# Linear attention with an MLP on one core: the feature map as min(exp, max(x + 1, 1)) and a new order of work in batches 0, 2 and 3

## The chip, the cores and the metric

The kernel runs on one core of one Trainium2 chip. The metric is the device time of one execution in microseconds (us); where several executions are given, the median counts. One further execution was taken by the hardware profiler, and all lines of profile below come from it. The engines are named as in the profile: PE is the matrix engine (PEld its weight loads), DVE the vector engine, ACT the scalar engine, POOL is GpSimd, and SP the queue that issues most of the transfers (DMA).

## The reference

```python
def phi(x):
    return np.where(x > 0, x, np.exp(x) - 1.0) + 1.0
q_p, k_p = (phi(q), phi(k))                    # q, k, v: 8 batches, 8 heads, 576 x 64
kv = np.einsum('bhsd,bhse->bhde', k_p, v)
z = np.sum(k_p, axis=2)
num = np.einsum('bhsd,bhde->bhse', q_p, kv)
den = np.einsum('bhsd,bhd->bhs', q_p, z)[..., None] + 1e-06
x = num / den                                  # then 4608 tokens x 512
h = x @ w_in                                   # 512 x 2048
g = 0.5 * h * (1.0 + np.tanh(c * (h + 0.044715 * h * h * h)))
out = g @ w_out                                # 2048 x 512
```

The feature map phi(x) is x + 1 for positive x and exp(x) otherwise. Two ways to write it matter here: max(x, 0) + min(exp(x), 1), and min(exp(x), max(x + 1, 1)). For positive x, exp(x) is above x + 1; for others, exp(x) is at most 1.

## The kernel before

**Tiles.** The 576 tokens of a batch are split into a main part of 512 tokens, held as 128 partitions with C = 4 chunks each, and a rest of 64. The rests of two batches share a tile of 128 partitions (k_r, v_r, q_r). The main tile of q, k or v is `[128, 8 heads, 4 x 64]` in fp32: within a head, the four chunks lie side by side. The feature maps k_p and q_p are `[128, 4, 8, 64]` in bf16: a chunk with all its heads is contiguous, because matmuls and transposes take pairs of heads (128 columns) of one chunk. All tiles loaded from memory, batches and weights alike, rotate through six buffers (`pld`, tag "ld"). A new load waits until the tile six loads back is read for the last time.

**Attention of a batch.** `exp_main` (L164) or a piece like L341 stores exp(x) in bf16 on ACT, in the layout of the input. `phi_into` (L169) does the rest on the DVE: one minimum with 1 over exp (L171), then for each chunk one operation with two tensor inputs, max(x, 0) + e (L175). `cast_v` (L202) puts v in bf16 beside a column of ones, `cast_vr` (L208) the rest of v. `kv_mm` (L213) multiplies k_p by v for each of four pairs of heads, five matmuls a pair. The ones' column gives z. `kv_evac` (L234) copies the result from PSUM into block-diagonal matrices (kvbd). q_p is transposed, on PE (L247, L336) or by a DMA transpose (`qtr`), and `nab_mm` (L251) forms numerator and denominator in one. `nab_evac` (L260) takes the reciprocal and multiplies (x, bf16). x is transposed once more into xt, the input of the first layer: by PE and a copy (`pe_tx`, L374 to L383) in batches 0 to 2, by a DMA transpose (`tx`, L487) in later ones.

**The two layers.** For each main part j of 512 tokens, and a ninth part made of all rests, `first_half(j)` (L657) runs m = 0 to 15: four matmuls of 128x512 for 128 hidden units (`first_mm`, L301) and a gelu on ACT (L675). Then `second_half(j)` (L703) runs 16 slots of four matmuls (L718) and copies outputs out. `first_mm_early` (L310) does the first 256 tokens of one m ahead of its time, at the end of the stage before, into a PSUM buffer; `first_half` then does the other 256.

**The order of work.** It is written out by hand. Each engine runs its instructions in the order of the program. `at(phase, j, slot, fn)` appends a function to a list that is run after slot `slot` of first_half(j) (phase 1) or second_half(j) (phase 2); functions of one slot run in the order in which they were appended. `plan_second`, `plan_third` (L586) and `plan_prepare` with `plan_attention` place the attention of batches 1, 2 and 3 to 7 so: batch 2 is prepared within second_half(1), batch 3 from second_half(1) to first_half(2). exp and gelu use different tables of ACT, so a stretch of exps has a table load at both ends.

**The head.** Batch 0 has no layer work to lie beside. PE is fed with filler matmuls there (`keep_warm(n)`, L325: 2n matmuls of 252 columns on zeros). The code from L339 to L407 gives the order: four exps for halves of the heads of k and q, `phi_into` for the same halves, `transpose_q` 0 and 1, fillers, the rest of k (`phi_rest_half`), casts of v, `transpose_q` 2 and 3, fillers, then twice `kv_mm` for two pairs and `kv_evac`. Between the two rounds stand two casts of v (L358, L359). `kv_evac` copies one half on the DVE, the other on ACT, one after the other.

**PSUM.** Two pools: `ps_ho` with four buffers of a bank (h_ps, o_ps, fillers, some transposes) and `ps_a` with two buffers of two banks (kv_ps, n_ps, and in j < 2 the first-layer results of m = 12 to 15, two to a buffer, L665 to L668). Both rotate in order of allocation. A matmul into a buffer waits for the reader of what was in it.

Of the kernel before, what the change touches and what calls it, by code (L numbers as in the profile page):

```python
# [15 lines left out]
def kernel(  # L16
# [17 lines left out]
    C = 4  # L34
# [128 lines left out]

    def exp_main(name, b):  # L164
        e = pe.tile([P, H, C * D], BF16, name=name + "_e")
        nc.scalar.activation(e, ld[name, b], AF.Exp)  # L166
        return e

    def phi_into(xp, x, e, hs):  # L169

        nc.vector.tensor_scalar(e[:, hs], e[:, hs], 1.0, None, op0=ALU.min)  # L171
        xv = x.rearrange("p h (c d) -> p c h d", d=D)
        ev = e.rearrange("p h (c d) -> p c h d", d=D)
        for c in range(xp.shape[1]):
            nc.vector.scalar_tensor_tensor(  # L175
                xp[:, c, hs, :], xv[:, c, hs, :], 0.0, ev[:, c, hs, :],
                op0=ALU.max, op1=ALU.add,
            )

    def phi_of(x, e, name):  # L180
        xp = pphi.tile([P, x.shape[2] // D, H, D], BF16, name=name)
        phi_into(xp, x, e, slice(0, H))
        return xp

    def phi_rest(name, m):
        x = ld[name, m]
        e = pe.tile([P, H, D], BF16, name=f"{name}_e{m % 2 if name == 'qr' else ''}")
        nc.scalar.activation(e, x, AF.Exp)
        return lambda: phi.__setitem__((name, m), phi_of(x, e, name + "_p"))

    def exp_rest_half(name, e, s):
        r = slice(REST * s, REST * (s + 1))
        nc.scalar.activation(e[r], ld[name, 0][r], AF.Exp)

    def phi_rest_half(name, e, s):
        r = slice(REST * s, REST * (s + 1))
        nc.vector.tensor_scalar(e[r], e[r], 1.0, None, op0=ALU.min)
        nc.vector.scalar_tensor_tensor(
            phi[name, 0][r, 0], ld[name, 0][r], 0.0, e[r], op0=ALU.max, op1=ALU.add
        )  # L200
# [114 lines left out]
    ke = pe.tile([P, H, C * D], BF16, name="k_e")  # L315
    qe = pe.tile([P, H, C * D], BF16, name="q_e")
    kre = pe.tile([P, H, D], BF16, name="kr_e")
# [21 lines left out]
    for n, e in (("k", ke), ("q", qe)):  # L339
        for s in halves:  # L340
            nc.scalar.activation(e[:, s], ld[n, 0][:, s], AF.Exp)  # L341
    exp_rest_half("kr", kre, 0)
    keep_warm(36)
    for n, xp, e in (("k", kp, ke), ("q", qp, qe)):
        for s in halves:
            phi_into(xp, ld[n, 0], e, s)
# [4 lines left out]
    cast_v(0, nc.scalar.copy, halves[0])  # L351
    cast_vr(0, (0,))
    for i in range(2, NP):
        transpose_q(i, nc.scalar.copy)
    keep_warm(2)
    for h in range(2):
        if h == 1:
            cast_v(0, nc.vector.tensor_copy, slice(4, 6))  # L358
            cast_v(0, nc.scalar.copy, slice(6, 8))  # L359
# [36 lines left out]
    kre1 = pe.tile([P, H, D], BF16, name="kr_e")  # L396
# [125 lines left out]
    def plan_second():  # L522
# [4 lines left out]
        def exps():  # L527
            box["q"] = pe.tile([P, H, C * D], BF16, name="q_e")
            for s in halves:
                nc.scalar.activation(box["q"][:, s], ld["q", b][:, s], AF.Exp)  # L530
            gelu_table()

        def phis():
            phi["q", b] = pphi.tile([P, C, H, D], BF16, name="q_p")
            for s in halves:
                phi_into(phi["q", b], ld["q", b], box["q"], s)
# [49 lines left out]
    def plan_third():  # L586
# [4 lines left out]
        def exps():  # L591
            box["k"] = exp_main("k", b)
            box["kr"] = phi_rest("kr", 1)
            box["q"] = exp_main("q", b)
# [28 lines left out]
        def tx(c):  # L623
            copy = nc.scalar.copy if c < 2 else nc.vector.tensor_copy
            pe_tx(b, c, box["x", c], c < 2, copy)

        def early(m):
            first_mm_early(2, m)

        at(1, 1, 10, cast_vs)  # L630
        at(1, 1, 11, exps)
        at(2, 1, 0, lambda: phis("k"))
        at(2, 1, 0, lambda: box["kr"]())
        at(2, 1, 0, lambda: phis("q"))
        at(2, 1, 0, qtr)
        at(1, 2, 3, lambda: box["qr"]())
        for i in range(NP):
            at(2, 1, 8 + i // 2, lambda i=i: kv(i))
        at(2, 1, 9, lambda: kv_evac(b, box["kv"]))
        for fn, c, slot in (  # L640
            (nab, 0, 10), (nab, 1, 11), (nab, 2, 12), (nab, 3, 13), (tx, 0, 13),
            (tx, 1, 14), (tx, 2, 15), (early, 0, 15), (tx, 3, 15), (early, 1, 15),
        ):
            at(2, 1, slot, lambda fn=fn, c=c: fn(c))
# [149 lines left out]
```

## Time and profile before

| What | us |
|---|---|
| Median of 8 executions | 297.07 |
| Lowest and highest of the 8 | 295.77, 299.12 |
| The profiled execution, its own time | 295.77 |
| Its span, first to last instruction | 294.0 |
| PE busy | 285.3 (97%) |
| ACT busy | 159.6 (54%) |
| DVE busy | 132.3 (45%) |
| POOL busy | 37.4 (13%) |

Times within the profile count from the span's start. What lies around the span is 1.77 us. A busy share is an average over stages. To find what sets the end one reads the chain of work that ended last, and then the stage in question. A line of a timeline gives the start and the length of a run of like instructions, engine, source line, operation, output <- inputs and their shapes (partitions x elements), the count, and in brackets how long the engine had been idle before it and what ended that. A line of the windows' table gives a stretch and its length, and then the busy us and instructions of each engine.

### The profile page before, as it was taken

The numbers are of one execution on the slowest core, as the hardware profiler recorded it, in microseconds if no ns is written. First come the engines' busy times: TensorE is split into PE (matmuls) and PEld (weight loads), VectorE is DVE, ScalarE is ACT, GpSimd is POOL, SyncE is SP. The second block draws the span as 40 slices with busy tenths as digits, with TensorE's granted clock in tenths as the row PEclk, the third lists the DMA queues.
The fourth block names the chain that finished last, engine by engine and source line by source line (L and its number), as shares of the span: only waits on it lengthen the run. The fifth ranks groups of instructions, "written<-read, shape, count | busy, mean of one in ns | idle before, by whom it ended". The sixth has DMA issues, their size and how long they took to land.

```text
span 294.0 us, 4289 instructions
## 1 busy us (share of the span) xinstructions
PE 285.3 (97%) x1669; PEld 149.5 (51%) x1698; DVE 132.3 (45%) x244; ACT 159.6 (54%) x222; POOL 37.4 (13%) x56
## 2 busy tenths in 40 slices
PE   8979999999999999999999999999999999999995
PEld 6856455644565544544454445544544444444443
DVE  2969494327689588346524592347242000000002
ACT  4749943579955762667355925682560076017400
POOL 8047658300001500000000000000000000000000
PEclk9999999999999999999999999999999999999999
DMA  7999999991498999739923797304231110021032
GB/s 250 352 380 405 394 382 371 318 382 59 102 328 257 205 274 321 174 62 281 304 78 71 235 302 144 64 10 125 89 56 36 71 71 2 0 93 50 2 71 72
DMA packets 64260, 53.24 MB, mean 181 GB/s; under 512 B 31728, under 2 KB 57584, under 8 KB 64240
## 3 DMA queue, kind: packets, MB, share of 16 engines
q1 hardware_dynamic: 60816, 41.82, 48.8%
q10 hardware_dynamic: 2464, 8.52, 7.6%
q0 software_dynamic: 960, 2.62, 3.6%
q8 instruction: 13, 0.21, 0.3%
q14 instruction: 7, 0.06, 0.1%
HBM read 36.70 MB, written 9.44 MB: 157 GB/s over the span
## 4 chain that ended last, share of the span: by engine, by line
PE 91%; DVE 5%; issue 1%; DMA 1%; ACT 1%; DVEq 0%
PE h_ps L301 42%; PE o_ps L718 40%; PE n_ps L253 3%; PE kv_ps L219 2%; DMA k_x<-in_k_dram 1%; PE o_ps L687 1%; PE t_ps L276 1%; DVE q_p L175 1%; DVE k_p L175 1%; DVE kvbd L242 1%; DVE x L265 1%; PE kv_ps L226 1%; DVE k_e L171 0%; ACT k_e L341 0%; PE t_ps L247 0%
## 5 line engine op out<-in xcount | busy, mean ns | idle before, releaser
L718 PE MATMUL o_ps<-w_out_sb,g 128*128 128x512 bf16 x545 | 123.5, 379 | 0.8
L301 PE MATMUL h_ps<-xt,w_in_sb 128*128 128x512 bf16 (+1 forms) x535 | 118.8, 364 | 0.8
L675 ACT ACTIVATE g<-h_ps 128x512 bf16<-128x512 f32 x144 | 83.7, 598 | 48.2 <-PE h_ps L301 45.6
L718 PEld LDWEIGHTS <-g 128*128 128x128 bf16 x560 | 54.1, 98 | 62.6
L301 PEld LDWEIGHTS <-w_in_sb 128*128 128x128 bf16 x612 | 57.7, 98 | 54.7 <-issue 0.5
L733 ACT COPY o_sb<-o_ps 128x512 f32<-128x512 f32 x18 | 10.5, 585 | 56.6 <-PE o_ps L718 56.6
L731 DVE COPY o_sb<-o_ps 128x512 f32<-128x512 f32 x17 | 11.7, 688 | 62.4 <-PE o_ps L718 62.3
L265 DVE TENSOR_TENSOR x<-n_ps,r 128x512 bf16<-128x512 f32 x36 | 24.9, 691 | 1.2
L175 DVE SCALAR_TENSOR_TENSOR q_p<-q_x,q_e 128x512 bf16<-128x512 f32 (+1 forms) x40 | 24.1, 663 | 0.3
L175 DVE SCALAR_TENSOR_TENSOR k_p<-k_x,k_e 128x512 bf16<-128x512 f32 (+1 forms) x36 | 22.0, 674 | 0.3
L242 DVE CAST kvbd<-kv_ps 64x260 bf16<-64x260 f32 (+1 forms) x16 | 6.5, 409 | 28.0 <-PE kv_ps L226 27.9
L171 DVE TENSOR_SCALAR k_e<-k_e 128x2048 bf16<-128x2048 bf16 (+1 forms) x9 | 6.7, 741 | 27.6 <-ACT k_e L166 22.9
L263 DVE RECIPROCAL r<-n_ps 128x8 f32<-128x8 f32 x36 | 7.4, 206 | 24.6 <-PE n_ps L253 24.6
L328 PE MATMUL w_ps<-warm 128*128 128x252 bf16 x94 | 13.7, 310 | 1.1 <-DVE warm L127 1.1
L301 PE MATMUL h_ps<-xt_rest,w_in_sb 128*128 128x512 bf16 x63 | 13.9, 379 | 0.1
L253 PEld LDWEIGHTS <-qt 128*128 128x128 bf16 x128 | 9.7, 98 | 7.9 <-issue 1.1
L166 ACT ACTIVATE k_e<-k_x 128x2048 bf16<-128x2048 f32 x7 | 13.4, 1910 | 0.2
L253 PE MATMUL n_ps<-kvbd,qt 128*128 128x130 bf16 x128 | 12.7, 221 | 0.6 <-ACT kvbd L242 0.3
L219 PEld LDWEIGHTS <-k_p 128*128 128x128 bf16 x128 | 9.7, 96 | 6.8 <-issue 1.4
L219 PE MATMUL kv_ps<-vp,k_p 128*128 128x130 bf16 x128 | 12.1, 220 | 0.9 <-DVE vp L203 0.8
L145 ACT ACT_TABLE_LOAD x8 | 10.3, 1283 | 4.6 <-DVE o_sb L731 4.5
L328 PEld LDWEIGHTS <-warm 128*128 128x128 bf16 x94 | 10.3, 112 | 3.1 <-DVE warm L127 1.1
(58 smaller groups left out, 146.0 us busy)
## 6 DMA issues: line engine op xcount, KB each, us to landing
out_dram<-o_sb ACTq DMA_DIRECT2D x16, 512.0 KB, 3.8
k_x<-in_k_dram SPq DMA_DIRECT2D x7, 1024.0 KB, 6.4
v_x<-in_v_dram SPq DMA_DIRECT2D x7, 1024.0 KB, 12.3
q_x<-in_q_dram SPq DMA_DIRECT2D x6, 1024.0 KB, 8.1
w_st<-in_moe_w_out_dram SPq DMA_DIRECT2D x4, 1024.0 KB, 10.9
w_st<-in_moe_w_in_dram SPq DMA_DIRECT2D x3, 1024.0 KB, 9.2
q_x<-in_q_dram SPq DMA_DIRECT2D x4, 512.0 KB, 9.1
k_x<-in_k_dram SPq DMA_DIRECT2D x2, 512.0 KB, 4.2
```

What stands on the lines that cost most here:

```text
L145: nc.scalar.preload_act_table_set("gelu_apprx_tanh_and_others")
L166: nc.scalar.activation(e, ld[name, b], AF.Exp)
L175: nc.vector.scalar_tensor_tensor(xp[:, c, hs, :], xv[:, c, hs, :], 0.0, ev[:, c, hs, :], op0=ALU.max, op1=ALU.add,)
L219: nc.tensor.matmul(dst, lhsT=kp[:, c, P * i : P * (i + 1)], rhs=vps[b % 2][:, 2 * i : 2 * i + 2, c, :], start=(c == 0), stop=False,)
L253: nc.tensor.matmul(n_ps[rows, i // 2, 2 * E * (i % 2) : 2 * E * (i % 2) + 2 * E], lhsT=qt_c[:, i, rows], rhs=kvbd[:, i, :], skip_group_che ...
L265: nc.vector.tensor_tensor(x, n_v[:, :, :, 0:D], r[:, :, :, None].to_broadcast([P, 2, 4, D]), op=ALU.mult,)
L301: nc.tensor.matmul(h_ps[:, tok], lhsT=w_in_sb[:, c, P * m : P * (m + 1)], rhs=xt[:, c, tok], start=(c == 0), stop=(c == KM - 1), skip_grou ...
L328: nc.tensor.matmul(w_ps[:, 0:252], lhsT=warm[:, 0:P], rhs=warm)
L675: nc.scalar.activation(gs[j][:, i, :], ps, AF.Gelu_apprx_tanh)
L718: nc.tensor.matmul(o_pss[t], lhsT=g[:, m, P * t : P * (t + 1)], rhs=w_out_sb[:, m, :], start=(m == 0), stop=(m == MM - 1),)
L731: nc.vector.tensor_copy(dst, o_ps)
L733: nc.scalar.copy(dst, o_ps)
```

## The change

- **The feature map.** ACT stores exp by chunk, in the layout of the feature map (`exp_into`). On the DVE, `phi_line` writes max(x + 1, 1) into the feature map in one operation, from fp32 to bf16, over all chunks, and `phi_min` takes the minimum of it and exp in place. The minimum over exp and the four operations by chunk (L171, L175; for the rest L197 and L198) are gone.
- **The head.** The casts of both halves of v stand ahead of the first `kv_mm`, each half shared by DVE and ACT (two heads each). The copy of `transpose_q` 3 is done by the DVE instead of ACT.
- **Batch 2** (`plan_third`). Exp of q comes ahead of exp of k. The feature map of q and its DMA transposes come ahead of k's. `kv_mm` runs at slots 5 and 6 of second_half(1) instead of 8 and 9, `nab` at 8 to 11 instead of 10 to 13. x is transposed by four DMA transposes from SP instead of PE and copies. Four `first_mm_early` instead of two stand at slot 15.
- **Batch 3.** q's feature map and its DMA transposes come at slot 15 of second_half(1), ahead of k's and v's cast (slots 0 and 1 of first_half(2)). Before, k came at slot 15, v at 0 and q at 1. `kv_mm` moves from slots 5 to 8 to slots 7 to 10.
- **Loads of batch 4** move from slot 2 to slot 12 of second_half(1).

```diff
@@ -161,43 +161,51 @@
 
     phi = {}
 
+    def by_chunk(x):
+        return x.rearrange("p h (c d) -> p h c d", d=D)
+
+    def exp_into(e, x, hs=slice(0, H)):
+        nc.scalar.activation(
+            e[:, :, hs, :].rearrange("p c h d -> p h c d"), by_chunk(x[:, hs]), AF.Exp
+        )
+
     def exp_main(name, b):
-        e = pe.tile([P, H, C * D], BF16, name=name + "_e")
-        nc.scalar.activation(e, ld[name, b], AF.Exp)
+        e = pe.tile([P, C, H, D], BF16, name=name + "_e")
+        exp_into(e, ld[name, b])
         return e
 
-    def phi_into(xp, x, e, hs):
-
-        nc.vector.tensor_scalar(e[:, hs], e[:, hs], 1.0, None, op0=ALU.min)
-        xv = x.rearrange("p h (c d) -> p c h d", d=D)
-        ev = e.rearrange("p h (c d) -> p c h d", d=D)
-        for c in range(xp.shape[1]):
-            nc.vector.scalar_tensor_tensor(
-                xp[:, c, hs, :], xv[:, c, hs, :], 0.0, ev[:, c, hs, :],
-                op0=ALU.max, op1=ALU.add,
-            )
+
+    def phi_line(xp, x, hs=slice(0, H)):
+        nc.vector.tensor_scalar(
+            xp[:, :, hs, :].rearrange("p c h d -> p h c d"), by_chunk(x[:, hs]),
+            1.0, 1.0, op0=ALU.add, op1=ALU.max,
+        )
+
+    def phi_min(xp, e, hs=slice(0, H)):
+        nc.vector.tensor_tensor(
+            xp[:, :, hs, :], xp[:, :, hs, :], e[:, :, hs, :], op=ALU.min
+        )
 
     def phi_of(x, e, name):
         xp = pphi.tile([P, x.shape[2] // D, H, D], BF16, name=name)
-        phi_into(xp, x, e, slice(0, H))
+        phi_line(xp, x)
+        phi_min(xp, e)
         return xp
 
     def phi_rest(name, m):
         x = ld[name, m]
-        e = pe.tile([P, H, D], BF16, name=f"{name}_e{m % 2 if name == 'qr' else ''}")
-        nc.scalar.activation(e, x, AF.Exp)
+        e = pe.tile([P, 1, H, D], BF16, name=f"{name}_e{m % 2 if name == 'qr' else ''}")
+        exp_into(e, x)
         return lambda: phi.__setitem__((name, m), phi_of(x, e, name + "_p"))
 
     def exp_rest_half(name, e, s):
         r = slice(REST * s, REST * (s + 1))
-        nc.scalar.activation(e[r], ld[name, 0][r], AF.Exp)
+        exp_into(e[r], ld[name, 0][r])
 
     def phi_rest_half(name, e, s):
         r = slice(REST * s, REST * (s + 1))
-        nc.vector.tensor_scalar(e[r], e[r], 1.0, None, op0=ALU.min)
-        nc.vector.scalar_tensor_tensor(
-            phi[name, 0][r, 0], ld[name, 0][r], 0.0, e[r], op0=ALU.max, op1=ALU.add
-        )
+        phi_line(phi[name, 0][r], ld[name, 0][r])
+        phi_min(phi[name, 0][r], e[r])
 
     def cast_v(b, fn, s=slice(0, H)):
         fn(
@@ -312,9 +320,9 @@
         hs[j, m] = ps_ho.tile([P, MAIN], FP32, name="h_ps", tag="ho")
         first_mm(j, m, hs[j, m], slice(0, MAIN // 2))
 
-    ke = pe.tile([P, H, C * D], BF16, name="k_e")
-    qe = pe.tile([P, H, C * D], BF16, name="q_e")
-    kre = pe.tile([P, H, D], BF16, name="kr_e")
+    ke = pe.tile([P, C, H, D], BF16, name="k_e")
+    qe = pe.tile([P, C, H, D], BF16, name="q_e")
+    kre = pe.tile([P, 1, H, D], BF16, name="kr_e")
     kp = pphi.tile([P, C, H, D], BF16, name="k_p")
     qp = pphi.tile([P, C, H, D], BF16, name="q_p")
     phi["k", 0], phi["q", 0] = kp, qp
@@ -338,25 +346,25 @@
 
     for n, e in (("k", ke), ("q", qe)):
         for s in halves:
-            nc.scalar.activation(e[:, s], ld[n, 0][:, s], AF.Exp)
+            exp_into(e, ld[n, 0], s)
     exp_rest_half("kr", kre, 0)
     keep_warm(36)
     for n, xp, e in (("k", kp, ke), ("q", qp, qe)):
         for s in halves:
-            phi_into(xp, ld[n, 0], e, s)
+            phi_line(xp, ld[n, 0], s)
+            phi_min(xp, e, s)
     for i in range(2):
         transpose_q(i, nc.scalar.copy)
     keep_warm(5)
     phi_rest_half("kr", kre, 0)
-    cast_v(0, nc.scalar.copy, halves[0])
     cast_vr(0, (0,))
     for i in range(2, NP):
-        transpose_q(i, nc.scalar.copy)
+        transpose_q(i, nc.scalar.copy if i == 2 else nc.vector.tensor_copy)
     keep_warm(2)
     for h in range(2):
-        if h == 1:
-            cast_v(0, nc.vector.tensor_copy, slice(4, 6))
-            cast_v(0, nc.scalar.copy, slice(6, 8))
+        cast_v(0, nc.vector.tensor_copy, slice(4 * h, 4 * h + 2))
+        cast_v(0, nc.scalar.copy, slice(4 * h + 2, 4 * h + 4))
+    for h in range(2):
         kv_ps = ps_a.tile([P, 2, 512], FP32, name="kv_ps", tag="a")
         for i in range(2):
             kv_mm(0, 2 * h + i, kv_ps, i)
@@ -393,7 +401,7 @@
     keep_warm(1)
     tx0(1)
     ke1 = exp_main("k", 1)
-    kre1 = pe.tile([P, H, D], BF16, name="kr_e")
+    kre1 = pe.tile([P, 1, H, D], BF16, name="kr_e")
     exp_rest_half("kr", kre1, 1)
     gelu_table()
     nab0(3)
@@ -525,15 +533,16 @@
         box = {}
 
         def exps():
-            box["q"] = pe.tile([P, H, C * D], BF16, name="q_e")
+            box["q"] = pe.tile([P, C, H, D], BF16, name="q_e")
             for s in halves:
-                nc.scalar.activation(box["q"][:, s], ld["q", b][:, s], AF.Exp)
+                exp_into(box["q"], ld["q", b], s)
             gelu_table()
 
         def phis():
             phi["q", b] = pphi.tile([P, C, H, D], BF16, name="q_p")
             for s in halves:
-                phi_into(phi["q", b], ld["q", b], box["q"], s)
+                phi_line(phi["q", b], ld["q", b], s)
+                phi_min(phi["q", b], box["q"], s)
 
         def cast_vs():
             cast_vr(0, (1,))
@@ -589,9 +598,9 @@
         box = {}
 
         def exps():
+            box["q"] = exp_main("q", b)
             box["k"] = exp_main("k", b)
             box["kr"] = phi_rest("kr", 1)
-            box["q"] = exp_main("q", b)
             box["qr"] = phi_rest("qr", 0)
             gelu_table()
 
@@ -621,27 +630,28 @@
             box["x", c] = nab_evac(n_ps)
 
         def tx(c):
-            copy = nc.scalar.copy if c < 2 else nc.vector.tensor_copy
-            pe_tx(b, c, box["x", c], c < 2, copy)
-
-        def early(m):
-            first_mm_early(2, m)
+            if c == 0:
+                xts[b] = pt.tile([P, NP, MAIN], BF16, name="xt")
+            nc.sync.dma_start_transpose(
+                out=xts[b][:, :, P * c : P * (c + 1)],
+                in_=box["x", c].rearrange("p a t d -> p (a t d)"),
+            )
 
         at(1, 1, 10, cast_vs)
         at(1, 1, 11, exps)
+        at(2, 1, 0, lambda: phis("q"))
+        at(2, 1, 0, qtr)
         at(2, 1, 0, lambda: phis("k"))
         at(2, 1, 0, lambda: box["kr"]())
-        at(2, 1, 0, lambda: phis("q"))
-        at(2, 1, 0, qtr)
         at(1, 2, 3, lambda: box["qr"]())
         for i in range(NP):
-            at(2, 1, 8 + i // 2, lambda i=i: kv(i))
-        at(2, 1, 9, lambda: kv_evac(b, box["kv"]))
-        for fn, c, slot in (
-            (nab, 0, 10), (nab, 1, 11), (nab, 2, 12), (nab, 3, 13), (tx, 0, 13),
-            (tx, 1, 14), (tx, 2, 15), (early, 0, 15), (tx, 3, 15), (early, 1, 15),
-        ):
-            at(2, 1, slot, lambda fn=fn, c=c: fn(c))
+            at(2, 1, 5 + i // 2, lambda i=i: kv(i))
+        at(2, 1, 6, lambda: kv_evac(b, box["kv"]))
+        for c, slot in enumerate((8, 9, 10, 11)):
+            at(2, 1, slot, lambda c=c: nab(c))
+            at(2, 1, slot, lambda c=c: tx(c))
+        for m in range(4):
+            at(2, 1, 15, lambda m=m: first_mm_early(2, m))
 
     def store(j, t, o_sb):
         if j < B:
@@ -739,9 +749,9 @@
     plan_second()
     plan_third()
     plan_prepare(
-        3, (2, 1, 7), (2, 1, 15), None, (1, 2, 0), (1, 2, 1), None, (2, 1, 12)
+        3, (2, 1, 7), (1, 2, 0), None, (1, 2, 1), (2, 1, 15), None, (2, 1, 12)
     )
-    plan_attention(3, 1, 2, (5, 6, 7, 8), (12, 13, 14, 15))
+    plan_attention(3, 1, 2, (7, 8, 9, 10), (12, 13, 14, 15))
     for b in range(4, B):
         j = b - 2
         plan_prepare(
@@ -753,7 +763,7 @@
     at(1, 2, 8, lambda: box0["qr"]())
     plan_rest(1, (2, 2, 8), (1, 3, 14))
     for b in range(4, B):
-        at(2, b - 3, 2 if b == 4 else 0, lambda b=b: load_batch(b))
+        at(2, b - 3, 12 if b == 4 else 0, lambda b=b: load_batch(b))
     for m in range(2, 4):
         at(2, 2 * m - 3, 3, lambda m=m: load_rests(m, (("kr", k), ("vr", v))))
         at(1, 2 * m - 2, 9, lambda m=m: load_rests(m, (("qr", q),)))
```

## The prediction

> **What bounds the kernel now.** I read the granted clock first (0.998, nothing throttles), then the shares of the chain that ended last, the busy time by stage, the timelines of the first 18 us, and those around batch 2. The first lines are that chain's shares and five stages of the busy-time table: stretch, its length, then busy us (and instructions) of PE, PEld, DVE, ACT, POOL, then clock, DMA share and GB/s.
>
> ```profile
> PE 91%; DVE 5%; issue 1%; DMA 1%; ACT 1%; DVEq 0%
> ...
> 4.50:14.30 9.80, 9.70 (x90) 8.33 (x89) 8.47 (x23) 7.13 (x9) 2.31 (x6) 1.00 1.10 356
> 14.30:18.00 3.70, 2.29 (x30) 1.81 (x28) 1.26 (x5) 1.76 (x5) 2.26 (x3) 1.00 1.08 382
> 18.00:21.00 3.00, 2.43 (x32) 1.69 (x29) 2.82 (x8) 1.19 (x3) 0.91 (x1) 1.00 1.12 369
> 21.00:53.00 32.00, 31.69 (x213) 18.05 (x215) 23.34 (x35) 21.50 (x30) 21.36 (x22) 1.00 1.07 384
> ...
> 67.00:86.60 19.60, 19.22 (x133) 10.94 (x134) 14.89 (x29) 16.55 (x20) 0.00 (x0) 1.00 0.48 138
> ```
>
> From 21 us on the matrix engine is full: a faster DVE gains nothing there unless PE work goes or a PE wait ends. In 4.5 to 14.3 PE looks full too, but that is filler (w_ps matmuls); the DVE, 8.47 of 9.80 us, sets the pace. So two places can move the end: the head, and the 19.6 us of batch 2's stage, where PE stands idle some 0.4 us and does removable work.
>
> The DVE and ACT timelines of the head (start, length, engine, line, operation, count, idle before it):
>
> ```profile
> 9.84 1.06 ACT L341 ACTIVATE q_e<-q_x 128x1024 bf16<-128x1024 f32 x1 [1.51 <-DMA q_x<-in_q_dram]
> ...
> 11.52 0.42 DVE L171 TENSOR_SCALAR q_e<-q_e 128x1024 bf16<-128x1024 bf16 x1
> 11.97 1.43 DVE L175 SCALAR_TENSOR_TENSOR q_p<-q_x,q_e 128x256 bf16<-128x256 f32 x4
> 13.32 0.28 DVE L197 TENSOR_SCALAR kr_e<-kr_e 64x512 bf16<-64x512 bf16 x1
> ...
> 15.93 0.62 ACT L203 CAST vp<-v_x 128x512 bf16<-128x512 f32 x1
> 17.41 0.26 ACT L242 CAST kvbd<-kv_ps 64x130 bf16<-64x130 f32 x1 [0.86 <-DVE kvbd L242]
> ```
>
> The last quarter of exp is ready at 10.90, but the DVE gives q_p only at 13.40. Then a cast of v sits behind kv's first copy: the cast at 15.93 holds kv's last pair until 16.60 in the chain, and the numerator matmul of batch 0 goes on at 17.73.
>
> Batch 2's stage, on ACT and PE:
>
> ```profile
> 71.79 2.06 ACT L675 ACTIVATE g<-h_ps 128x512 bf16<-128x512 f32 x4
> ...
> 74.85 0.40 PE L219 MATMUL kv_ps<-vp,k_p 128*128 128x130 bf16 x4
> ...
> 78.08 0.39 PE L253 MATMUL n_ps<-kvbd,qt 128*128 128x130 bf16 x4 [0.19 <-DVE kvbd L242]
> ```
>
> The four gelus are those of m = 12 to 15, held up by batch 2's four exps (65.73 to 70.48) and a table load on either side; kv comes after them; the numerator follows kv by one slot and waits for its copy.
>
> **What the Trainium skill says.** The Trainium skill, "VectorE: DVE Perf Modes", The perf-mode tier table: for 2048 elements tensor_scalar takes 693 ns in bf16 and 1227 in fp32, tensor_tensor in bf16 1224, in fp32 2293. The trace agrees where it has a row: minimum on bf16 128x2048 689 ns, cast fp32 to bf16 with a strided output 1222. It has no bf16 tensor_tensor in SBUF; I take the page's price. "SBUF — State Buffer", Who interferes with whom: a DVE operation with two SBUF inputs, or in a two-port mode, excludes GpSimd's reads. The trace fits: 128x512 STTs take 0.69 us alone, 1.05 (4.18 for four) beside POOL's casts at 24.2. "TensorE: Matmul & The Clock Gate", Part 1, engine queue depths: matmuls stay in program order, only weight loads go ahead. So a kv matmul that waits holds all the second-layer matmuls behind it.
>
> **The feature map.** Half of heads, before: 0.42 + 1.43, paced 1.80 us (9.71, 11.52, 13.32). After, two operations, which I call line (add 1, max 1, on fp32 x) and min (of that and exp, both bf16). Line 128x1024, between casts of 512 at 0.41 and 2048 at 1.22: 0.68; min 0.68 at the page's rate. Pair 1.32 to 1.37. The line no longer needs exp. The full tensor: 0.72 + 2.50 = 3.1 before, 2.4 after. Bounds of the pair 128x2048: 2.4 with both at two per cycle, 3.5 with min at one (2.29), 4.6 with both at one. The first is taken, since the cast row has the same types and layout. Exp stored by chunk costs ACT nothing: the cast of v on ACT, strided too, has 1.06 for 1024 elements, as exp.
>
> **Head, step by step** (clock of before). Loads stay: DMA share is above 1.05 throughout and exp of q's second half waited for its load until 9.84. DVE: line q 9.84 to 10.52, min 10.92 to 11.6 (before 13.40), the rest of k 11.5 to 12.37 (0.41 each from the vr cast), vr to 12.7. PE: filler ends 11.38, eight transposes of 0.056 and ten fillers of 0.107 to 12.9, the last eight to 13.35. Copies: third on ACT 13.3 to 13.9, fourth on DVE 13.55 to 13.97. Casts: DVE (0.41) ends 14.29 and 14.61, ACT (0.62, paced 0.53) 14.43 and 14.96. These four are now ahead of both kv copies. kv runs 14.34 to 15.46, four pairs of 0.28. From last kv matmul to numerator was 16.84 to 17.73 = 0.87 to 0.89; so the last pair's at 15.40 gives 16.27, against 17.73: **1.46 us earlier**. After that, the same DVE chain of reciprocal and multiply.
>
> Does it reach the dense part? The weights come at the pace of the loads and of POOL's casts. The first-layer matmuls of m = 8 begin at 28.25 (24.8 plus four groups of 0.86) and would now need their quarter of w_in at 26.8; POOL casts it from 25.13 (four in 5.18) to 26.4. The gelus of m = 0 on begin at 24.85 still, since k of batch 1 arrives at 20.96; fast enough. The tightest for w_out, rows of m = 4 and 5: cast from 35.60, half of 2.47, out at 36.83; needed at slot 4 of second_half(0), 35.1 + 4 x 0.86 - 1.46 = 37.1. Batch 1's v lands at 41.61, its cast ends 42.84, needed at 45.42 - 1.46 = 43.96. All hold, by 0.2 to 1.1; so the 1.46 is kept, and more than about 1.7 could not be.
>
> **Batch 2's stage** (before's clock, second_half(1) from 67.08, a slot 0.863). Removed: 16 PE transposes, 0.056 each: -0.89. The wait before the numerator (it starts 0.57 after the matmul before it, where 0.22 is the pace) goes, since two slots now lie between: -0.35. The wait of the first-layer matmuls for the last x copy (DVE 84.86 to 85.28; PE goes on at 85.34, the matmul before began at 84.99 and needs 0.11) goes: -0.24. Four early half-matmul groups instead of two: 128x256 keeps 0.108 apiece, so nothing. Added: kv at slot 5, due at 67.08 + 6 x 0.863 = 72.26. Its PSUM buffer is released by gelu 12 and 13, at 71.79 + 0.49 + 0.60 = 72.88: **+0.66**, and behind it in PE's queue stand all second-layer matmuls. Its other inputs: min q ends 68.9 (exp q at 67.64), k 71.2 (exp k ends 69.44), the rest 72.0: in time. The four q transposes leave SP from 69.0 instead of 73.22, land by 75.3, needed 76.7. Sum **-0.83**.
>
> The four x transposes go to SP, issue 1.2, landing 2.4 after issue: numerator at 76.7, 77.8, 78.9, 79.9, x 1.4 later, landed 80.5, 81.6, 82.7, 83.8. First-layer work needs the first two at 83.6 (slot 15's end) and the others at 85.4: covered by 1.6 to 2.0 us. They stand ahead of load_batch(4), now at slot 12, so SP issues those loads at 82.5 instead of 78.49; they took 6, 10.5 and 14 us, landing by about 97, and are read from 102.3: nothing. No queue is blocked by them, DMA being at 0.11 of its time in 70 to 75.
>
> Batch 3: q at slot 15, then k and v. DVE 83.4 + 2.4 + 2.4 + 1.2 = 89.1; kv, now at slot 7, is due at 90.5: nothing, with 1.4 to spare. Its q transposes leave from 86, contended by the loads, needed at 96. Later batches: no PE wait to remove; nothing.
>
> **Sum**: -1.46 - 0.83 = -2.29. The profiled execution took 295.77 us (span 294.0 and 1.77 around it), so 293.5; it was the lowest of the eight, 1.30 under their median. On the median: 297.07 - 2.29 = **294.8**.
>
> **Rivals.** (1) Min runs at one element per cycle. The head barely feels it (line runs ahead while q loads; gain 1.35), but batch 2's chain of min q, k, rest ends 74.5 against 72.5, 2.05 instead of 0.66 lost, and batch 3's v cast comes 0.95 late: -1.35 + 0.57 + 0.95 = +0.2, no change, 297.2. For it: no row shows the operation. Against: the page. (2) Both at one per cycle: the pair costs 4.6 us against 3.2. kv of batch 0 begins 2.2 us later than forecast (+0.75 against before), batch 2's kv waits 3.4 (net +1.9), batch 3's 3.2: +5.9, **303, slower**. It turns from gain to loss at a pair of about 3.5 us, between (1) and the forecast. Against: the 1222 ns cast. (3) x transposes late: batch 3's landed 5.2 to 6.2 us after issue where loads ran beside them; so here, PE would wait about 1.5: 296.3. For: batch 4's loads stand right behind. Against: they are behind. (4) The head's gain is eaten by weights and casts coming at their old time: only 0.83 left, 296.2.
>
> **Chances.** Forecast 0.65, its own range 293.4 to 295.6 (the 0.66 absent; or some of the head lost); (1) 0.09; (2) 0.06; (3) 0.10; (4) 0.10. A measurement here tells about 0.5%, 1.5 us, from no change. Faster, below 295.6: the forecast and a little of (3) and (4), 0.68. Within: 0.24, slower 0.08. The range, 293.2 to 297.0, leaves out (2) and part of (1).
>
> **What would show it.** Min rows at 1.2 us for 128x2048 and line rows likewise; q_p done near 11.6; batch 0's numerator near 16.3; dense PE from 19.5; kv of batch 2 waiting about 0.7 for a gelu; no PE transposes of x there; no PE gap at the start of first_half(2). It is wrong if min rows show 2.3, if PE waits for weights between 24 and 40, or if first-layer matmuls of batch 2 wait for DMA.

## The result, and the profile after

The changed kernel takes **306.61 us** (median of 11 executions, 304.45 to 308.84) against 297.15 before (32 executions): a ratio of 1.0315, 95% interval 1.0287 to 1.0342. It is slower, where the forecast was 2.3 us faster. The profiled execution took 306.08 us, its span is 304.3, against 295.77 and 294.0. The ratios leave disturbed executions out, so they can differ a little from those of the medians, and for one kernel below (batch 4's loads on ACT's queue at slot 14) the profiled execution is itself such a one.

First the chain that ended last, by engine, from the page of the kernel after. Before, PE held 91% of it and DMA 1%.

```profile
PE 74%; DMA 15%; ACT 4%; SPq 3%; issue 1%; DVE 1%; POOL 0%; ACTq 0%
```

Then PE's waits in the kernel after (what waited, for what: us in all, times, longest).

```profile
PE n_ps L261 <- DMA qt<-q_p: 7.9, 1, 7.9
PE h_ps L309 <- DMA xt<-x: 1.2, 1, 1.2
...
PE o_ps L728 <- POOL w_out_sb L156: 0.9, 1, 0.9
...
PE kv_ps L227 <- ACT g L685: 0.5, 1, 0.5
```

One wait of 7.9 us makes most of the loss: numerator matmuls that wait for a DMA transpose of q_p. The stages, in the columns of the table shown of before (stretch and its length, busy us and instructions of PE, PEld, DVE, ACT and POOL, granted clock, DMA share, GB/s):

```profile
4.50:14.30 9.80, 9.42 (x87) 8.04 (x85) 7.59 (x14) 6.70 (x9) 3.02 (x6) 1.00 1.08 328
...
21.00:53.00 32.00, 30.81 (x201) 17.07 (x203) 15.51 (x24) 21.53 (x30) 18.07 (x20) 1.00 1.07 385
...
67.00:86.60 19.60, 17.79 (x116) 9.85 (x117) 13.27 (x20) 14.45 (x16) 0.00 (x0) 1.00 0.47 114
86.60:106.00 19.40, 11.43 (x76) 6.59 (x77) 5.29 (x10) 7.44 (x13) 5.40 (x8) 0.89 1.13 256
```

The last row is the place, and the prediction put no cost on it. The same stretch of the kernel before:

```profile
86.60:106.00 19.40, 19.25 (x120) 9.91 (x122) 14.27 (x27) 13.84 (x19) 5.40 (x8) 1.00 0.99 238
```

PE goes from 19.25 to 11.43 us busy, and the DMA share from 0.99 to 1.13. So before, with a share of 0.99, the transfer engines had hardly any time to spare here, just behind the stage that the change works on. Which wait it was, on PE's timeline of after:

```profile
95.38 1.89 PE L309 MATMUL h_ps<-xt,w_in_sb 128*128 128x512 bf16 x7
105.13 0.62 PE L261 MATMUL n_ps<-kvbd,qt 128*128 128x130 bf16 x4 [7.86 <-DMA qt<-q_p]
```

It is the first numerator of batch 3, which in the kernel before needs no wait:

```profile
96.87 0.40 PE L253 MATMUL n_ps<-kvbd,qt 128*128 128x130 bf16 x4
```

And SP's timeline of after, around the loads of batch 4:

```profile
77.77 5.12 SPq L635 DMA_TRANSPOSE xt<-x  x4
82.94 0.71 SPq L67 DMA_DIRECT2D k_x<-in_k_dram  x1
83.75 0.82 SPq L67 DMA_DIRECT2D q_x<-in_q_dram  x1
84.66 2.12 SPq L67 DMA_DIRECT2D v_x<-in_v_dram  x1
86.88 15.79 SPq L463 DMA_TRANSPOSE qt<-q_p  x4
```

against the same in the kernel before:

```profile
78.49 0.58 SPq L67 DMA_DIRECT2D k_x<-in_k_dram  x1
79.17 0.52 SPq L67 DMA_DIRECT2D q_x<-in_q_dram  x1
79.78 1.08 SPq L67 DMA_DIRECT2D v_x<-in_v_dram  x1
90.95 5.59 SPq L455 DMA_TRANSPOSE qt<-q_p  x4
```

Before, 10 us lie between the loads and batch 3's q transposes; after, nothing does, and the issue of four transposes takes 15.79 us instead of 5.59. The landings, read from the records of the single transfers:

| | loads k, q, v of batch 4 landed | q transposes of batch 3 landed | needed |
|---|---|---|---|
| before | 84.49, 89.62, 93.73 | 94.36, 95.06, 97.89, 99.87 | 96.87, 97.97, 99.06, 100.16 |
| after | 90.54, 95.47, 103.61 | 105.09, 106.17, 106.53, 106.99 | 97.27 (the first) |

Even before, the third and fourth transposes landed only 1.2 and 0.3 us ahead of their matmuls.

**The span's 10.3 us, by marks on PE** (the numerator is due where its matmul begins less the wait before it, 105.13 - 7.86):

| Mark | Before | After | Difference | Since the mark above |
|---|---|---|---|---|
| first-layer work begins | 20.95 | 19.57 | -1.38 | -1.38 |
| second_half(1) begins | 67.08 | 66.73 | -0.35 | +1.03 |
| numerator of batch 3 due | 96.87 | 97.27 | +0.40 | +0.75 |
| the same, begins | 96.87 | 105.13 | +8.26 | +7.86 |
| second_half(2) begins | 100.39 | 110.39 | +10.00 | +1.74 |
| end of the span | 294.0 | 304.3 | +10.3 | +0.3 |

### The profile page after: what moved, and what is told of

The parts are those of the page before. It is cut to its first block, busy times and chain, and to the rows that moved or that the text cites. A ratio compares the mean times of both kernels' runs of the same rounds, so it can differ in the third digit from the quotient of the medians.

```text
span 304.3 us, 4211 instructions
## 1 busy us (share of the span) xinstructions
PE 285.9 (94%) x1661; PEld 149.7 (49%) x1690; DVE 113.0 (37%) x187; ACT 157.4 (52%) x219; POOL 35.9 (12%) x56
## 4 chain that ended last, share of the span: by engine, by line
PE 74%; DMA 15%; ACT 4%; SPq 3%; issue 1%; DVE 1%; POOL 0%; ACTq 0%
PE o_ps L728 35%; PE h_ps L309 32%; DMA qt<-q_p 6%; DMA w_st<-in_moe_w_out_dram 4%; DMA k_x<-in_k_dram 3%; PE n_ps L261 3%; PE kv_ps L227 2%; SPq L67 2%; DMA xt<-x 2%; ACT k_e L168 1%; PE o_ps L697 1%; SPq L90 1%; ACT L145 1%; ACT q_e L168 1%; SPq L76 1%
## 5 line engine op out<-in xcount | busy, mean ns | idle before, releaser
L309 PEld LDWEIGHTS <-w_in_sb 128*128 128x128 bf16 x620 | 58.8, 98 | 56.0 <-DMA xt<-x 1.5
L168 ACT ACTIVATE k_e<-k_x 128x2048 bf16<-128x2048 f32 (+1 forms) x9 | 15.5, 1719 | 4.8 <-DMA k_x<-in_k_dram 4.7
L168 ACT ACTIVATE q_e<-q_x 128x2048 bf16<-128x2048 f32 (+1 forms) x10 | 15.6, 1561 | 3.4 <-DMA q_x<-in_q_dram 3.4
L185 DVE TENSOR_TENSOR k_p<-k_p,k_e 128x2048 bf16<-128x2048 bf16 (+1 forms) x9 | 10.5, 1171 | 12.8 <-ACT k_e L168 12.5
L211 DVE CAST vp<-v_x 128x2048 bf16<-128x2048 f32 (+1 forms) x9 | 9.3, 1045 | 9.8 <-DMA v_x<-in_v_dram 9.8
L179 DVE TENSOR_SCALAR q_p<-q_x 128x2048 bf16<-128x2048 f32 (+1 forms) x10 | 10.1, 1010 | 7.2 <-DMA q_x<-in_q_dram 7.1
```

The lines of the kernel that those rows point to most:

```text
L168: nc.scalar.activation(e[:, :, hs, :].rearrange("p c h d -> p h c d"), by_chunk(x[:, hs]), AF.Exp)
L179: nc.vector.tensor_scalar(xp[:, :, hs, :].rearrange("p c h d -> p h c d"), by_chunk(x[:, hs]), 1.0, 1.0, op0=ALU.add, op1=ALU.max,)
L185: nc.vector.tensor_tensor(xp[:, :, hs, :], xp[:, :, hs, :], e[:, :, hs, :], op=ALU.min)
L309: nc.tensor.matmul(h_ps[:, tok], lhsT=w_in_sb[:, c, P * m : P * (m + 1)], rhs=xt[:, c, tok], start=(c == 0), stop=(c == KM - 1), skip_grou ...
```

## The experiments

**Theory**: the move of batch 4's loads from slot 2 to slot 12, behind batch 2's new x transposes, puts 3 MB straight before batch 3's q transposes. **Rivals**: the new order within batch 3 is to blame; or SP's queue alone, so that another queue would cure it; or the new feature map and head would cost the time even without the moves.

**The loads' slot, earlier and later.** In the kernel after:

```diff
-        at(2, b - 3, 12 if b == 4 else 0, lambda b=b: load_batch(b))
+        at(2, b - 3, 2 if b == 4 else 0, lambda b=b: load_batch(b))
```

> The changed kernel with one edit: batch 4's loads back at slot 2 of second_half(1). Theory A (batch 3's q transposes stand in SP's queue behind batch 4's 3 MB, so PE waits 8.0 us for them and then runs 2.3 us slower at half clock): the loads are through by about 88, so that wait goes, -10.3; but batch 2's x transposes now stand behind the loads instead, PE waits some 2 to 4 us for them: 298 to 300. Rival B (the order q before k in batch 3 is what makes them late): about 306 still.

Measured: 304.16, ratio to before 1.0211 (1.0165 to 1.0256). PE's longest wait in this kernel:

```profile
PE h_ps L309 <- DMA xt<-x: 6.4, 1, 6.4
```

The wait for batch 3's q is gone (landed 93.68 to 97.56); it is now batch 2's x, as expected, but 6.4 us long where 2 to 4 were expected. Those transposes were issued 79.16 to 88.7, behind loads that landed 81.58, 84.29 and 87.02, and landed themselves at 87.59 to 93.15. Later, with 15 in place of 12:

> The changed kernel with one edit: batch 4's loads at slot 15 of second_half(1), in SP's queue behind batch 3's q transposes. Theory A: transposes land by 93, no wait of 8.0 us, no half clock, and the 1.4 us wait for batch 2's last x transpose goes too; 306.6 - 10.3 - 1.4 = 294.9, with 1 us more if k of batch 4 comes late for its exp. Rival B: 306. Rival C (the 16 DMA engines are shared, the queue does not matter): transposes issued at 87 still run beside output stores and POOL's loads: 298 or more.

Measured: 303.89, 1.0191 (1.0136 to 1.0245). PE's longest wait:

```profile
PE n_ps L261 <- DMA qtr<-qr_p: 5.4, 1, 5.4
```

Now both sets of transposes pass, and the next one in SP's queue is caught, so that the 294.9 that was expected is missed: the transpose of the rests' q, issued at 96.58 behind loads that landed until 108.26, landed at 108.86. So three slots give three victims; slots 2 and 15 are 2.4 and 2.7 us below the kernel after by their medians, and none gives the time back.

**The loads left out.** This kernel leaves out part of the work: batch 4 reads batch 3's q, k and v again, and its 3 MB are never loaded.

```diff
     def load_batch(b):
+        if b == 4:
+            for n in ("k", "q", "v"):
+                ld[n, b] = ld[n, 3]
+            return
```

> The changed kernel without the loads of batch 4; its attention reads batch 3's q, k and v again, so 3 MB of loads are left out. If those loads are what holds batch 3's q transposes (and batch 2's last x transpose), both waits go, 8.0 + 1.4, and the half clock after the first, 2.3: 306.6 - 11.7 = 295. If output stores and POOL's loads of the rests are enough to hold them, PE still waits 2 to 4 us: 298 to 300.

Measured: 296.01 (20 executions), 0.9957 (0.9937 to 0.9978). The q transposes of batch 3 landed at 90.14 to 96.65 and no PE wait names them. All else being as in the kernel after, these loads cost 10.6 us there. This time also lacks their traffic, so it is a bound and not a version. That stores and rests alone would hold the transposes, the other possibility named, is ruled out.

**The order within batch 3.** Its old order back (k and v first, q later, kv in slots 5 to 8), the loads still at slot 12:

```diff
-        3, (2, 1, 7), (1, 2, 0), None, (1, 2, 1), (2, 1, 15), None, (2, 1, 12)
+        3, (2, 1, 7), (2, 1, 15), None, (1, 2, 0), (1, 2, 1), None, (2, 1, 12)
...
-    plan_attention(3, 1, 2, (7, 8, 9, 10), (12, 13, 14, 15))
+    plan_attention(3, 1, 2, (5, 6, 7, 8), (12, 13, 14, 15))
```

> The changed kernel with batch 3 in its old order (k at slot 15, v and q after, kv at slots 5 to 8); batch 4's loads stay at slot 12. Theory A: the transposes are issued at about 90, still behind the loads that land at 90 to 103: PE still waits 6 to 9 us, 304 to 307. Rival B (q first is what makes them late): 297.

Measured: 305.59, 1.0297 (1.0251 to 1.0343). PE's longest wait:

```profile
PE n_ps L261 <- DMA qt<-q_p: 6.5, 1, 6.5
```

The transposes leave at 89.30 instead of 86.88 and land from 103.62 all the same: they are held by the loads, whenever they leave. The rival of the order falls.

**Another queue.** Batch 4's loads from ACT's queue:

```diff
-            ld[n, b] = load_main(src, b, n + "_x", nc.sync)
+            ld[n, b] = load_main(src, b, n + "_x", nc.scalar if b == 4 else nc.sync)
```

> The changed kernel with one edit: batch 4's three loads at the same slot, but issued from ACT's queue instead of SP's. Theory A (order within SP's queue): the transposes no longer stand behind the loads, land before 97, and the time falls to 296 to 298. Rival C (sharing of the 16 engines): transposes still land at 103 to 105, 305 to 307.

Measured: 300.56, 1.0101 (1.0043 to 1.0159). Better by 6 us than after, still slower than before, and between the two values that were expected. ACT's timeline shows that the loads did not leave where the program has them:

```profile
74.14 1.91 ACT L168 ACTIVATE k_e<-k_x 128x2048 bf16<-128x2048 f32 x1
74.20 0.40 ACTq L67 DMA_DIRECT2D k_x<-in_k_dram  x1
74.64 0.59 ACTq L67 DMA_DIRECT2D q_x<-in_q_dram  x1
75.28 1.86 ACTq L67 DMA_DIRECT2D v_x<-in_v_dram  x1
75.95 1.89 ACT L168 ACTIVATE q_e<-q_x 128x2048 bf16<-128x2048 f32 x1
```

ACT's queue hands out the transfers 8.7 us earlier than SP's did, before ACT has gone through the work of the slots between. So they met batch 2's x transposes:

```profile
PE h_ps L309 <- DMA xt<-x: 4.0, 1, 4.0
```

What counts for the theory: SP issued these from 77.08 to 82.7 with no delay of its own (5.67 us for four), and they landed at 84.34 to 87.50, 6.1 us or more after issue, when the loads on the other queue were nearly through (86.65). SP's order is therefore not the whole cause. That agrees with the Trainium skill, "DMA: Bandwidth & Descriptors", Issuing engines are not separate DMA queues: transfers of all issuers run on the same 16 engines and interleave.

SP's order is a part of the cause, though. The records of the single packets (3 MB of loads are 3072 packets of 1 KB, a transpose has packets of 256 B) show when the first packet of the waiting transposes begins, and how many of the loads' packets are then still to come:

| Kernel | transposes issued from | their first packet | loads' packets still to come |
|---|---|---|---|
| after (same queue) | 86.88 | 98.55 | 231 |
| loads at slot 2 (same queue) | 79.16 | 85.83 | 97 |
| loads at slot 15 (same queue) | 96.58 | 106.61 | 213 |
| loads on ACT's queue | 77.08 | 81.20 | 1212 |

In one queue the transposes do not begin until over 90% of the loads' packets have; from two queues both run side by side, and the first transpose landed before the last load (84.34 against 86.65). The same loads placed later on that queue (slot 14):

> The changed kernel with batch 4's loads issued from ACT's queue at slot 14, so at about 82.5 to 85, the same time as in the changed kernel, but not in SP's queue. If order within SP's queue is what counts: batch 3's q transposes land by 93 to 96, no wait at the numerator: 296 to 298. If sharing of the 16 DMA engines is what counts: they land when the loads are through, at 98 to 104: 302 to 307.

Measured: 305.73 (four executions, 301.05 to 307.41); the ratio, 1.0185 (1.0121 to 1.0249), rests on two of them. Its trace is weak evidence: the loads left at 85.65 to 89.4, and the q transposes, issued on SP from 88.66, landed at 97.03 to 108.94. Two of the four were there before the last load (107.17), two behind it, which fits sharing; but also a 2.6 us wait of PE for an ACT copy appeared. I count this run as inconclusive.

**What the standstill costs beyond itself.** After the wait, PE's granted clock is 0.50 for a while. Fillers within the wait, which compute nothing of use:

```diff
+    at(1, 2, 11, lambda: keep_warm(36))
```

> The changed kernel with 72 filler matmuls (7.7 us at full clock) after slot 11 of first_half(2), where PE waits 8.0 us for the transposes. If the slow matmuls after the wait (0.43 us apiece instead of 0.22) come from PE having stood still, the filler fills the wait, costs nothing, and keeps the clock up: 306.6 - 2.3 = 304.3, and the 0.50 in the granted clock of 102 to 108 us is gone. If they have another cause, 306.6 or more.

Measured: 304.67, 1.0274 (1.0244 to 1.0304), 1.94 us below the kernel after. Compare the same stretch behind the wait, after (the first two us of it, then all six):

```profile
106.00:108.00 2.00, 2.00 (x9) 1.01 (x8) 0.76 (x2) 0.51 (x1) 0.00 (x0) 0.50 0.56 104
...
106.00:112.00 6.00, 6.00 (x32) 3.05 (x31) 3.86 (x8) 2.82 (x4) 0.00 (x0) 0.77 0.46 90
```

and with the fillers:

```profile
106.00:112.00 6.00, 5.84 (x42) 2.97 (x41) 3.86 (x9) 4.97 (x6) 0.00 (x0) 1.00 0.52 69
```

The mean granted clock is 0.77 in the one, with 0.50 at its start, and 1.00 in the other. From the first numerator of batch 3 to second_half(2) the kernel after takes 5.26 us; with the fillers it is 3.52 (104.66 to 108.18), the same as before. This accounts for the +1.74 of the table of marks.

**The half that needs no move.** The kernel before with the new feature map and the new head; batches 2 and 3 and the loads stay in the order of before:

```diff
-            phi_into(xp, ld[n, 0], e, s)
+            phi_line(xp, ld[n, 0], s)
+            phi_min(xp, e, s)
...
     for h in range(2):
-        if h == 1:
-            cast_v(0, nc.vector.tensor_copy, slice(4, 6))
-            cast_v(0, nc.scalar.copy, slice(6, 8))
+        cast_v(0, nc.vector.tensor_copy, slice(4 * h, 4 * h + 2))
+        cast_v(0, nc.scalar.copy, slice(4 * h + 2, 4 * h + 4))
+    for h in range(2):
```

> The kernel before with the new feature map and the new head alone; batches 2 and 3 and the loads of batch 4 as before. Theory A: the head's 1.37 us are there in the trace at the first dense matmul, but some of them go in the wait for w_out (1.0 in the profiled run): 295.8 to 296.8. Rival D (the feature map or the head costs time by itself): 298 or more.

Measured: 299.07 (20 executions, 295.91 to 301.90), 1.0019 (0.9990 to 1.0048): no gain, where 295.8 to 296.8 were expected, but no part of the 9.5 us either. The times fall in two groups, seven from 295.91 to 297.42 and thirteen from 298.77; the profiled execution (299.66) is of the upper one, and no trace shows whether the lower one has the waits below. In it the head's 1.57 us are there until batch 3's first numerator (95.30 against 96.87), and then are lost again, on PE:

```profile
97.13 0.41 PE L261 MATMUL n_ps<-kvbd,qt 128*128 128x130 bf16 x4 [0.57 <-DMA qt<-q_p]
...
99.55 0.41 PE L261 MATMUL n_ps<-kvbd,qt 128*128 128x130 bf16 x4 [1.15 <-DMA qt<-q_p]
...
102.05 0.61 PE L261 MATMUL n_ps<-kvbd,qt 128*128 128x130 bf16 x4 [1.23 <-DMA qt<-q_p]
```

The same transposes again, though the loads of batch 4 are where they were. What changed is on POOL. Its transfers of the next rests (1 MB), before:

```profile
94.17 1.35 POOL L76 DMA_DIRECT2D q_r<-in_q_dram  x2 [39.04 <-ACT g L675]
```

and in this kernel:

```profile
90.67 1.35 POOL L76 DMA_DIRECT2D q_r<-in_q_dram  x2 [35.09 <-DVE qr_p L185]
```

They wait for the buffer of an earlier q_r (the rests rotate in buffers of their own), which a faster DVE frees sooner: its last step there, qr_p, ends at 90.58 instead of 93.62 (the view of before names a gelu that ended 0.3 us behind it). So they now start 3.5 us earlier, of which 1.57 are the head's, beside the q transposes (issued 89.85 to 95.5), which land at 93.62 to 102.01 instead of 94.36 to 99.87. Behind these waits the granted clock falls to 0.50 as well, and the span ends 3.9 us later than before. The feature map alone, with the head in the old order, shows the same:

```diff
-        phi_into(xp, x, e, slice(0, H))
+        phi_line(xp, x)
+        phi_min(xp, e)
```

> The kernel before with the new feature map alone; head order, batches 2 and 3 and loads as before. If a shorter DVE alone is harmless, q_p of batch 0 is ready some 1.8 us sooner and part of it reaches the dense part: 296 to 297. If the shorter DVE frees the tiles of the rests sooner, POOL's loads start about 3 us sooner, meet batch 3's q transposes, and PE waits for those: 298 to 299, and the trace shows PE waiting for qt between 95 and 103.

Measured: 297.82 (13 executions, 296.94 to 301.06), 1.0049 (1.0020 to 1.0078); in the profiled execution, one of the longer ones (300.07), POOL's transfers from 91.73, and 2.8 us of wait for qt. A faster feature map alone makes this kernel 0.5% slower.

**Holding the rests back.** To test that, the rests' transfers are tied to batch 3's first reciprocal by a small POOL copy, in the kernel with map and head alone:

```diff
+            if b == 3 and c == 0:
+                nc.gpsimd.tensor_copy(out=gate, in_=last["r"])
...
-        at(1, 2 * m - 2, 9, lambda m=m: load_rests(m, (("qr", q),)))
+        at(1, 2 * m - 2, 12 if m == 2 else 9, lambda m=m: load_rests(m, (("qr", q),)))
```

> The kernel before with the new feature map and head, and one more edit: POOL's loads of the later rests (1 MB) are held until batch 3's first reciprocal, by a small POOL copy that reads it. In the same kernel without this, PE waited 3.4 us for batch 3's q transposes, with POOL's loads beside them, and took 299.1. If those loads are the cause, the wait goes and the head's 1.5 us show: 295.6. If the transposes are late for another reason (no time left after batch 4's loads), 298 to 299 as before.

Measured: 306.41, 1.0326 (1.0296 to 1.0356). A miss, and a useful one. What was to be tested holds: with the rests out of the way, batch 3's transposes landed 4.77, 3.87, 3.19 and 2.52 us after issue, where without the gate it was 3.77, 5.56, 6.67 and 7.87, and PE did not wait for them. But the rests (101.85 on) ran into batch 3's x transposes and batch 5's loads, and batch 4's q transposes, issued at 122.98, landed at 130.95. PE's longest waits:

```profile
PE n_ps L261 <- DMA qt<-q_p: 5.2, 1, 5.2
PE h_ps L313 <- POOL w_in_sb L149: 2.9, 1, 2.9
```

The wait for q transposes moved one batch on. That is not the whole loss: of the 11.9 us over the span of before, 8.2 arise behind the start of second_half(2) (104.14 against 100.39), and 3.75 ahead of it, where PE waited for w_in early on. Why w_in came late there was not traced.

**The change without the x transposes by DMA.** If the transfers have no room for one more set in this stretch, then the change without that part should do. This is the kernel after with x of batch 2 transposed by PE in the slots of before, and therefore kv in slots 8 and 9 and the loads back at slot 2:

```diff
         def tx(c):
-            if c == 0:
-                xts[b] = pt.tile([P, NP, MAIN], BF16, name="xt")
-            nc.sync.dma_start_transpose(
...
+            copy = nc.scalar.copy if c < 2 else nc.vector.tensor_copy
+            pe_tx(b, c, box["x", c], c < 2, copy)
...
-            at(2, 1, 5 + i // 2, lambda i=i: kv(i))
+            at(2, 1, 8 + i // 2, lambda i=i: kv(i))
...
-        at(2, b - 3, 12 if b == 4 else 0, lambda b=b: load_batch(b))
+        at(2, b - 3, 2 if b == 4 else 0, lambda b=b: load_batch(b))
```

> The kernel before with the new feature map, the new head and q first in batches 2 and 3 (q's transposes of batch 3 from slot 15 of second_half(1), kv at slots 7 to 10), but batch 2's x still transposed by PE and batch 4's loads still at slot 2. Theory A': what a queue of DMA work has no room for is batch 2's x; without it the loads start at 74 and are through by 88 to 90, batch 3's q transposes follow at once, land by 92 to 94, before POOL's loads of the rests fill the engines, and are needed at 95: no PE wait, head's 1.5 us kept: 295.6. If q first does not bring the transposes ahead of POOL's loads: 298 to 299, as with map and head alone.

Measured: **295.56** (14 executions, 293.86 to 296.86), 0.9941 (0.9917 to 0.9965) to before, and 11 us below the kernel after: faster than before by 0.6%, and as expected (295.6). SP's timeline:

```profile
74.93 0.58 SPq L67 DMA_DIRECT2D k_x<-in_k_dram  x1
75.62 0.52 SPq L67 DMA_DIRECT2D q_x<-in_q_dram  x1
76.25 1.41 SPq L67 DMA_DIRECT2D v_x<-in_v_dram  x1
87.60 5.47 SPq L463 DMA_TRANSPOSE qt<-q_p  x4
```

The loads landed at 80.71, 83.42 and 86.12, before the q transposes left; these landed at 90.94 to 95.89, needed from 96.66 on, with POOL's rests (91.95 on) only behind them. No PE wait names qt or xt. From the kernel after with its loads at slot 2 (304.16) it differs only in batch 2's x and the slots that go with it, so with the loads at that place the set of x transposes costs 8.6 us by the medians. This kernel and the one with map and head alone (299.07) differ only in the order of batches 2 and 3, q first here. So that order, which gained nothing in the kernel after, is what makes the faster map pay. By the traces it does so by putting the transposes ahead of the rests (the last issue 91.81, the first rest 91.95). The profiled executions of this kernel and of before differ by only 0.2 us (its q_p came 1.2 us late in that one, so its head gained 0.46); how the median's 1.5 us splits between head and waits was not traced.

## Why the prediction was wrong

**Right, by its own steps.** The prices: the line operation takes 1223 ns and min 1225 for 128x2048, in the groups by shape of the kernel after,

```profile
L185 DVE TENSOR_TENSOR q_p<-q_p,q_e 128x2048 bf16<-128x2048 bf16 x6 | 7.4, 1225 | 2.3 <-ACT q_e L168 1.8
L179 DVE TENSOR_SCALAR q_p<-q_x 128x2048 bf16<-128x2048 f32 x6 | 7.3, 1223 | 0.1
```

so the value taken from the Trainium skill, "VectorE: DVE Perf Modes", The perf-mode tier table (1224 for bf16 tensor_tensor, 1227 for fp32 tensor_scalar) holds, and rivals (1) and (2) fall. The head: q_p came at 12.39 where 11.6 was forecast, because the load of q came late (the line waited 0.79 for it, and exp began 0.77 later than before); but that was still ahead of 12.9, where the forecast has PE ready for the last transposes of it, and the casts' new place gave the numerator at 16.35 (forecast 16.27) and first-layer work 1.38 earlier (1.46). kv of batch 2 waited for the gelu as forecast: it starts at 72.59 where 71.91 would be its turn, 0.68 against 0.66, and the second-layer matmuls behind it go on only at 73.17.

```profile
72.59 0.39 PE L227 MATMUL kv_ps<-vp,k_p 128*128 128x130 bf16 x4 [0.51 <-ACT g L685]
```

Three of the forecast's figures are off without bearing on its sum: 0.72 + 2.50 is 3.2 and not 3.1; batch 3's DVE work ends at 89.4 by its terms and not 89.1, 1.1 ahead of kv; and of batch 3's x transposes only the first two took 5.2 to 6.2 us, the others 4.1 and 3.2.

**A part of rival (4).** "All hold, by 0.2 to 1.1" was too fine: w_out's load landed at 36.99 (35.54 before), PE waited at 38.14 for its cast, and 1.03 of the 1.38 were gone at second_half(1). Why that load came later was not tested; with the same head in the kernel with map and head alone it landed at 35.34, and PE did not wait for it there.

**A part of rival (3).** The x transposes of batch 2 did not all "land in time": the fourth, issued at 81.67, landed at 86.37, 4.70 us later, beside an output store of 82.40 and the load of k behind it (without the loads it took 3.79, and PE waited 0.3 us). PE waited 1.20 at first_half(2). That turns the forecast -0.83 into +0.75 for this stretch; of the difference of 1.58, the wait is 1.20; the rest, 0.38, was not followed further (0.24 of it was to be saved at this very spot).

**The step that failed** is this: "Its q transposes leave from 86, contended by the loads, needed at 96", with no cost. They landed from 105.09, PE waited 7.86 us, and the clock cost another 1.74. The prediction moved batch 3's transposes earlier by 4 us, moved batch 4's loads later by 4 us, and so pushed one into the other; it saw that they would be "contended" and put no number to it. The 5.2 to 6.2 us of batch 3's x transposes, beside which ran only the 1 MB of rests, would have had them there at about 92, in time. What it left out is the order in the queue: behind 3 MB on SP no transpose landed before those were through (in this kernel and with the loads at slots 2 and 15), and the prediction's own figure for that, about 97, was already past the need at 96. The loads then took longer too: the third landed 18.95 us after its issue instead of 13.95, at 103.61. New beside them were the rests (from 90.22, where they stood behind the loads before, at 94.17) and the last x transpose of batch 2; the 1 MB of stores ran beside them before as well. How much of the 5 us each of these makes was not tested. The check "DMA being at 0.11 of its time in 70 to 75" was made for the transposes of batch 2, and not for 85 to 105, where the same view had 0.78 to 1.14.

A second omission is that the prediction has no term for what a faster DVE sets off later: the rests' buffer comes free sooner and 1 MB starts 3.5 us earlier, into transposes with 0.3 us to spare. Map and head alone show it: the 1.57 us were gained and then lost.

**Theory at the end.** From about 68 to 106 us the transfers must carry three sets of four transposes of batches 2 and 3 and the single one of the rests, batch 4's 3 MB, 1 MB of stores and 1 MB of rests, each due within a few us. A fourth set, x of batch 2, was taken from PE (0.89 us of its time, by the forecast's price) and given to them. Shown: without the loads, or without that set and with the loads at slot 2, the 10 us are gone; with both, some transpose waits at every slot tried. Shown too: in SP's queue a transpose does not begin until nearly all of the loads ahead of it have, and from another queue it still shares the engines with them. Open: how many us the order and the sharing are worth each (the run at slot 14 did not settle it), whether x of batch 2 on PE would do with the loads left at slot 12, and why w_out came late.

## What to carry to other kernels

A transfer moved in a queue must be priced against the next transfer behind it that an engine will wait for: take from the trace how long it took to land, add that to the new start, and compare with the time at which the one behind it is needed. Read the DMA share in the stage after the one that is changed, and list how far ahead of its reader each transpose lands; one with 0.3 us to spare makes every speed-up elsewhere a risk. When an engine gets faster, ask which buffers it frees sooner and which transfers thereby start sooner.

## What the runs showed of the hardware

- A transpose alone lands 2.4 us after its issue. Behind 3 MB in the same queue, the first one took 18.2 us (86.88 to 105.09) and SP stood 6.32 us in its issue, against 1.2 to 1.3; its first packet began at 98.55, with 231 of the loads' 3072 still to come. With the loads on another queue it still took 6.1 to 8.0 us (77.08 to 84.34, 78.67 to 86.67).
- A transfer issued on ACT's queue can leave ahead of ACT's work that stands before it in the program (at 74.20 here, with the exps of batch 3's q and rest, placed five slots ahead of it, still to come). What released it at that moment was not traced.
- PE's last matmul before the standstill ended at 97.27. The granted clock was 1.00 in 98 to 100, 0.97 in 100 to 102, then 0.50 until 108 and 0.82 in 108 to 110, and matmuls of 512 columns followed each other at 0.43 us in place of 0.216; this cost 1.74 us by the marks and 1.94 by the medians with and without fillers. The Trainium skill, "TensorE: Matmul & The Clock Gate", Part 1, has an idle window of some 3.4 us for it. In the kernel with map and head alone the clock fell to 0.50 in 102 to 104 though no single wait was over 1.23 us: PE was busy 0.85 and 0.82 us in the two stretches of 2 us before. So a window without any work was not needed there; several short waits were enough.
